# Six decay tiles spread by one-hot products into PSUM, a third chunk of masked float32 scores, and products of zeros at the start

## The chip, the cores and the metric

The kernel runs on one core of one Trainium2 chip. The metric is the device time of one execution in microseconds (us). Before the change its median over 3 runs is 554.11 us (554.05 to 554.75).

## The reference

Three stages follow each other: a scan-like attention over 32 sequences (4 batches by 8 heads, 768 positions, head size 32, state size 16), and two feed-forward layers over its 3072 tokens of width 256.

```python
# attention, chunk by chunk
cum = np.cumsum(log_a, axis=-1)
L = np.exp(cum[:, :, :, None] - cum[:, :, None, :]) * causal      # decay between two positions
y = (C @ B.T * L) @ x + (C @ state) * np.exp(cum)                  # within the chunk, and from before
state = decay_full * state + sum_j(B_j x_j * decay_from_j)
# first layer: 256 -> 768 -> 256
h = max(x @ w1, x @ w2, x @ w3);   x1 = h @ w_out
# second layer: 256 -> 1536 -> 256
out = (sigmoid(x1 @ w_gate) * (x1 @ w_val)) @ w_out2
```

All operands are float32, and the weights arrive as pairs of 32-bit words (int64 views on the host) that are decoded on the chip.

## The kernel before, in words

**Attention.** The kernel uses chunks of 96 positions (8 chunks) and handles four sequences at a time, so one chunk has 8 steps g and the whole attention 64 steps k. Step k does this:

- TensorE makes the scores `s` of four sequences, four matmuls of 128x96 into one PSUM bank. In the first `FIRST` = 16 steps (two chunks) both operands are float32: the columns of C are masked by ScalarE (`act.mul(ck ...)`, line 327) so that only the wanted sequence remains, and each float32 matmul stands in the trace as two records (line 332). Later chunks use bf16 parts: `split_bc` (line 294) loads B and C of the chunk, cuts them into three bf16 terms (ScalarE's casts in line 303, GpSimd's subtractions in line 312), and 12 DMAs put these into the tiles `bi` and `cs` (line 308). The matmul is then in line 335.
- `dec` holds the decay factors. One tile serves two steps. It is loaded from DRAM into all 128 partitions by a broadcast DMA of 388 KB (`load_decay`, line 269) and turned into running products by two scans on VectorE (`decay`, line 291) against a 0/1 matrix `delta` that lies in PSUM.
- VectorE multiplies scores by decay into `mt` (line 347), GpSimd adds 16 columns for the state (line 340), and TensorE makes `y` from `mt` and `xs` (line 356).
- When four steps are done, ScalarE and VectorE cut `y` into a high and a low part (`xt_hi` line 366, `xt_lo` line 368), and four VectorE transposes (line 372) put the new state into `xs` of the next chunk.

The first two `dec` tiles come straight from the input and are clipped on VectorE (line 287). The others come from `ad`, a clipped copy in DRAM that `clip_all` writes (lines 261 and 264).

**First layer.** The tokens are handled in 6 tiles t of 512. For each of 6 blocks m, three products `u` (j = 0, 1, 2; lines 406 to 408, each with a high and a low part) go into three PSUM banks. ScalarE copies the first (line 484), VectorE takes the maximum with the second and the third (lines 486 and 488), and a high and low part of that goes into the two products `o`. Block m needs the weight pieces `a{m}0` and `a{m}1`, 512 KB each. A piece is decoded by three ScalarE operations (lines 165, 170, 174), one VectorE operation `t_a` (line 178), one on GpSimd (line 183), a ScalarE copy (line 211) and a GpSimd subtraction (line 213).

**What sets the order.** All DMAs go through SyncE's queue in the order of issue. `BEHIND` ties the load of weight pieces to the load of a certain `dec` tile. A tile of `dec` can only be loaded when one of its `DECS` = 4 buffers is free. Twelve attention steps (`START`) run before the first layer begins with tile t = 0; they yield its 512 tokens. The other steps are spread between the products of the first layer (`UNTIL`: 24 steps done by the end of t = 0). Inside these bounds a scheduler puts each engine's instructions into their final order, and every engine takes its own strictly one after the other.

Of the kernel before, what the change touches and what calls it, by code (L numbers as in the profile page):

```python
# [19 lines left out]
CH = 96  # L20
# [22 lines left out]
FIRST = 2 * NG  # L43
MASKED = 8
SHARED = 24
LEAD = 2
# [6 lines left out]
BEHIND = {4: 1, 5: 1, 6: 2, 7: 2, 8: 2, 9: 1, 10: 1, 11: 1, 12: 1}  # L53
# [18 lines left out]
def scan_attention_then_ffn(ctx: ExitStack, tc: tile.TileContext, xh, ah, bch, pick, bn, w1, w2, w3,  # L72
# [62 lines left out]

    todo = [(piece1, m, part) for m in range(M1) for part in range(2)]
# [7 lines left out]
    def load_weights():  # L144
# [4 lines left out]
        for k, s in enumerate(loads):  # L149
            sp.dma_start(out=raw[:, 2 * k:2 * k + 2].rearrange("p b n t -> p b (n t)"), in_=s)  # L150
        loaded.append((raw, wpool, blocks, name))

    def decode(raw, wpool, blocks, name):
# [23 lines left out]
        with behind(1):  # L177
            dve.scalar_tensor_tensor(out=t, in0=f1, scalar=3, in1=sg, op0=ALU.logical_shift_left,
                                     op1=ALU.bitwise_or)
# [73 lines left out]
    bcf = [flat[:, MASKED * 4 * CH + (BW + 384) * k:][:, 0:BW + 384] for k in range(2)]  # L253
    pk = acon.tile([128, NG], F32, name="pk")

    def clip_all():

        t = awk.tile([128, 2, LW], F32, tag="ac", bufs=1, name="ac")
        sp.dma_start(out=t.rearrange("p u w -> p (u w)"),
                     in_=ah.rearrange("r (s w) -> (r s) w", s=4))  # L260
# [3 lines left out]
        sp.dma_start(out=ad.rearrange("r (s w) -> (r s) w", s=4),  # L264
                     in_=t.rearrange("p u w -> p (u w)"))
# [17 lines left out]
    def decay(n, clip=False):  # L283

        t = dec[n]
        if clip:
            dve.tensor_scalar(out=t[:, :, 1:LW], in0=t[:, :, 1:LW], scalar1=1e-6, scalar2=1.0,
                              op0=ALU.max, op1=ALU.min)
        for h in range(PU // 4):
            f = t[:, 4 * h:4 * h + 4].rearrange("p u w -> p (u w)")  # L290
            dve.tensor_tensor_scan(out=f, data0=f, data1=delta.rearrange("p u w -> p (u w)"),  # L291
                                   initial=0.0, op0=ALU.mult, op1=ALU.add)

    def split_bc(c):
# [6 lines left out]
        for p in range(3):  # L301
            with tc.issue_after(evict[0].ins) if c > 2 else ExitStack():
# [18 lines left out]
    def attention(k, ahead):  # L321
# [24 lines left out]
        else:  # L346
            last[0] = dve.tensor_tensor(out=m[:, :, 0:CH], in0=ps[:, :, 0:CH], in1=dc[:, :, 1:LW],
# [5 lines left out]
        for i in [g] if k < START else (g, g - 3, g - 2, g - 1) if g % 4 == 3 else []:  # L353
# [428 lines left out]
```

## Time and profile before

| | |
|---|---|
| median of 3 runs | 554.11 us |
| profiled execution | 554.77 us, span 553.0 us, so 1.77 us lie around the span |
| TensorE busy | 535.5 us (97%) |
| VectorE busy | 384.0 us (69%) |
| ScalarE busy | 322.2 us (58%) |
| GpSimd busy | 128.2 us (23%) |
| DMA | 50.51 MB, mean 91 GB/s over the span |

The shares are means over stages that differ. The profile is therefore read by stage below: the attention's first 12 steps (6.6 to 35.4 us), the first tile of the first layer (39.1 to 85.4 us), and what follows. In the trace PE is TensorE's matmuls, DVE is VectorE, ACT is ScalarE, POOL is GpSimd and SP is SyncE; a "q" behind a name is the engine's instruction queue. A matmul's duration includes its way through the array, so the distance from one start to the next tells its price in a row of equal ones. The column PEclk is the granted TensorE clock as a share of 2.4 GHz; before the first clock record, at 43.06 us, it shows 1.00 whatever the clock was.

### The profile page before, as it was taken

The page shows a single profiled execution, that of the slowest core. Times are in us where ns is not written, and L with a number is a line of the kernel's source. Part 1 is how long each engine was busy: PE and PEld are TensorE (multiplying, and loading weights), DVE is VectorE, ACT ScalarE, POOL GpSimd, SP SyncE. Part 2 cuts the span into 40 slices and gives each one's busy share as a digit, 9 for nine tenths or more (in the row PEclk, how much of TensorE's full clock was granted, in tenths as well). Part 3 has the DMA queues.
Part 4 walks back from the last instruction along what each step waited for, and adds up shares of the span by engine and source line. Part 5 has one row for each costly group of instructions (what it writes and reads, how often), then busy time and mean ns, then how long its engine had stood idle before and what let it go on. Part 6 is the DMA issues. An engine that isn't in the chain of part 4 may idle for free.

```text
span 553.0 us, 7923 instructions
## 1 busy us (share of the span) xinstructions
PE 535.5 (97%) x2885; PEld 429.3 (78%) x2885; DVE 384.0 (69%) x648; ACT 322.2 (58%) x571; POOL 128.2 (23%) x161
## 2 busy tenths in 40 slices
PE   5998999999999999999999999999999999999997
PEld 5777667777677778888888878877888878888885
DVE  4988985676776834799988896586455567554554
ACT  5667745334335223687798886675555565555563
POOL 3568996555555430000000000000000000000000
PEclk9999899999999999999999999999999999999999
DMA  7999985894985118013220000001000002000002
GB/s 234 344 268 241 298 200 87 187 180 142 192 197 125 31 59 321 1 38 118 76 75 0 1 1 2 0 19 58 1 0 2 0 1 77 0 1 0 1 0 76
DMA packets 32150, 50.51 MB, mean 91 GB/s; under 512 B 3184, under 2 KB 18160, under 8 KB 32112
## 3 DMA queue, kind: packets, MB, share of 16 engines
q1 hardware_dynamic: 31824, 49.63, 34.1%
q8 instruction: 22, 0.36, 0.3%
q10 hardware_dynamic: 288, 0.39, 0.2%
q14 instruction: 16, 0.13, 0.1%
HBM read 38.51 MB, written 3.25 MB: 76 GB/s over the span
## 4 chain that ended last, share of the span: by engine, by line
PE 83%; DMA 9%; DVE 4%; ACT 1%; issue 1%; SPq 0%; DVEq 0%; ACTq 0%
PE o L659 17%; PE ug L628 15%; PE uv L628 15%; PE u L406 9%; PE u L408 8%; PE u L407 8%; DMA raw_a<-in_w 6%; PE o L407 3%; PE o L406 3%; PE o L408 3%; DMA dec<-ad 2%; PE y L356 2%; PE s L335 1%; DVE dec L291 1%; DMA ad<-ac 1%
## 5 line engine op out<-in xcount | busy, mean ns | idle before, releaser
L659 PE MATMUL o<-hi,w_d 128*128 128x512 f32 x288 | 97.6, 390 | 0.0
L406 PE MATMUL u<-xt_hi,w_a 128*128 128x512 f32 x216 | 88.4, 409 | 3.7 <-DVE s L488 2.6
L628 PE MATMUL ug<-xt_hi,w_g 128*128 128x512 f32 x252 | 91.5, 392 | 0.1
L628 PE MATMUL uv<-xt_hi,w_v 128*128 128x512 f32 x252 | 90.3, 390 | 0.0
L407 PE MATMUL u<-xt_lo,w_a 128*128 128x512 f32 x216 | 85.8, 397 | 0.1
L408 PE MATMUL u<-xt_hi,w_a 128*128 128x512 f32 x216 | 85.5, 396 | 0.0
L659 PEld LDWEIGHTS o<-hi,w_d 128*128 128x128 f32 x288 | 54.0, 188 | 11.3 <-ACT hi L702 0.2
L703 DVE TENSOR_TENSOR lo<-y,hi 128x512 fp32r<-128x512 f32 x72 | 49.4, 688 | 16.8 <-ACT hi L702 15.9
L291 DVE TENSOR_TENSOR_SCAN dec<-dec,delta 128x388 f32<-128x388 f32 x64 | 57.8, 945 | 1.3 <-DMA dec<-ad 1.1
L477 ACT CAST hi<-s 128x512 fp32r<-128x512 f32 x36 | 22.3, 621 | 61.5 <-DVE s L488 60.9
L659 PE MATMUL o<-lo,w_d 128*128 128x512 f32 x144 | 56.4, 391 | 0.8 <-DVE lo L703 0.8
L628 PEld LDWEIGHTS ug<-xt_hi,w_g 128*128 128x128 f32 x252 | 47.3, 188 | 12.1 <-ACT ug L631 0.9
L628 PEld LDWEIGHTS uv<-xt_hi,w_v 128*128 128x128 f32 x252 | 47.3, 188 | 10.6 <-DVE y L699 0.8
L406 PEld LDWEIGHTS u<-xt_hi,w_a 128*128 128x128 f32 x216 | 41.2, 191 | 13.7 <-POOL mt L340 1.7
L628 PE MATMUL ug<-xt_lo,w_g 128*128 128x512 f32 x126 | 49.1, 390 | 0.0
L628 PE MATMUL uv<-xt_lo,w_v 128*128 128x512 f32 x126 | 49.0, 389 | 0.0
L408 PEld LDWEIGHTS u<-xt_hi,w_a 128*128 128x128 f32 x216 | 41.4, 192 | 9.1
L407 PEld LDWEIGHTS u<-xt_lo,w_a 128*128 128x128 f32 x216 | 41.3, 191 | 8.4 <-DVE xt_lo L368 0.6
L702 ACT CAST hi<-y 128x512 fp32r<-128x512 f32 x72 | 44.4, 620 | 5.8 <-DVE y L699 4.4
L699 DVE TENSOR_TENSOR y<-uv,y 128x512 f32<-128x512 f32 x36 | 24.8, 688 | 30.9 <-PE uv L628 30.7
L486 DVE TENSOR_TENSOR s<-u,s 128x512 f32<-128x512 f32 x36 | 24.8, 688 | 24.6 <-PE u L408 19.4
L636 DVE TENSOR_TENSOR y<-ug,y 128x512 f32<-128x512 f32 x36 | 24.8, 690 | 24.4 <-ACT y L633 17.4
(103 smaller groups left out, 956.9 us busy)
## 6 DMA issues: line engine op xcount, KB each, us to landing
dec<-ad SPq DMA_DIRECT2D x30, 388.0 KB, 5.8
raw_a<-in_w SPq DMA_DIRECT2D x18, 256.0 KB, 6.9
bi<-parts SPq DMA_DIRECT2D x36, 128.0 KB, 5.3
cs<-parts SPq DMA_DIRECT2D x36, 96.0 KB, 5.5
xs<-in_xh SPq DMA_DIRECT2D x6, 512.0 KB, 5.0
raw_g<-in_wg SPq DMA_DIRECT2D x6, 512.0 KB, 5.0
raw_v<-in_wv SPq DMA_DIRECT2D x6, 512.0 KB, 5.9
raw_d<-in_wo SPq DMA_DIRECT2D x6, 512.0 KB, 4.3
```

Of the source, the lines that this page charges most:

```text
L291: dve.tensor_tensor_scan(out=f, data0=f, data1=delta.rearrange("p u w -> p (u w)"), initial=0.0, op0=ALU.mult, op1=ALU.add)
L406: pe.matmul(ps, wlo, a_hi(k), start=k == 0, stop=False)
L407: pe.matmul(ps, whi, a_lo(k), start=False, stop=False)
L408: pe.matmul(ps, whi, a_hi(k), start=False, stop=k == kn - 1)
L477: act.copy(hl[0], s)
L486: dve.tensor_tensor(out=s, in0=banks[1], in1=s, op=ALU.max)
L628: turn[0] = pe.matmul(ps, w, x, start=new and e == 0, stop=e == 2, skip_group_check=not new)
L636: evict[1] = dve.tensor_tensor(out=self.t[k], in0=ps, in1=self.t[k], op=ALU.add)
L659: turn[0] = pe.matmul(acc2[t][d], w, x, start=n == 1 and e == 0, stop=n == M2 and e == 2)
L699: evict[1] = dve.tensor_tensor(out=g, in0=v, in1=g, op=ALU.mult)
L702: act.copy(hl[0], g)
L703: dve.tensor_tensor(out=hl[1], in0=g, in1=hl[0].bitcast(F32), op=ALU.subtract)
```

## The change

Six things are changed.

1. The first six `dec` tiles (`SPREAD`, 12 half tiles) are no longer loaded by broadcast DMAs. The clipped factors stay in a tile `a4`, one row for each half tile. A float32 product with a one-hot column (`spread`) copies row h to all 128 partitions of a PSUM bank, and the scan reads it there. Two banks, those of the later `o`, take turns: the product h + 2 follows the scan of h.
2. `FIRST` is 24: the third chunk's scores, too, are made from masked float32 operands, so `split_bc` starts with the fourth chunk.
3. At the very start 12 products of zeros (`idle_products`, bf16, 128x512) stand ahead of all other TensorE work; they read `sg`, which GpSimd clears first (line 142). Eight more follow steps 9, 10 and 11.
4. The weight pieces a00 and a01 are loaded ahead of the first `dec` tile that is still loaded, and two pieces ride behind each of the tiles 6 to 10.
5. VectorE's first decode operations are tied to attention steps (`AFTER`), and the `dec` tiles 6 and 7 are scanned after the twelfth step (`LATER`).
6. One step's state transposes are moved behind the low part of step 11, and `y` is made after each single step up to step 24.

```diff
-FIRST = 2 * NG
+FIRST = 3 * NG
+LATER = START // 2
+IDLE0 = 12
+IDLE = {9: 3, 10: 3, 11: 2}
+AFTER = {"a00": 6, "a01": 7, "a10": 11}
+SPREAD = 6
...
-BEHIND = {4: 1, 5: 1, 6: 2, 7: 2, 8: 2, 9: 1, 10: 1, 11: 1, 12: 1}
+BEHIND = {6: 2, 7: 2, 8: 2, 9: 2, 10: 2}
...
-        with behind(1):
-            dve.scalar_tensor_tensor(out=t, in0=f1, scalar=3, in1=sg, op0=ALU.logical_shift_left,
+        with behind(1) if second else tc.issue_after(mts[AFTER.get(name, -1)].ins):
+            mts[name] = dve.scalar_tensor_tensor(out=t, in0=f1, scalar=3, in1=sg,
...
+    a4 = acon.tile([128, 4, LW], F32, name="a4")
...
+        t = a4[0:NC * NP * 2]
+        dve.memset(a4[NC * NP * 2:128], 0.0)
...
+    def spread(h):
+
+        ps = pso.tile([128, TT], F32, tag=f"o{h % 2}", name=f"spread{h}")
+        pe.matmul(ps[:, 0:4 * LW], delta_s[:, 3, h + 1:h + 2].to_broadcast([128, 128]),
+                  a4.rearrange("p u w -> p (u w)"), start=True, stop=True)
+        spreads.append(ps)
...
-    def load_decay(n, src):
+    def load_decay(n):
         t = awk.tile([128, PU, LW], F32, tag="dec", bufs=DECS, name=f"dec{n}")
-        i = sp.dma_start(out=t.rearrange("p u w -> p (u w)"), in_=src[n].partition_broadcast(128))
         dec[n] = t
+        if n < SPREAD:
+            return
+        i = sp.dma_start(out=t.rearrange("p u w -> p (u w)"), in_=ad[n].partition_broadcast(128))
...
-        if clip:
-            dve.tensor_scalar(out=t[:, :, 1:LW], in0=t[:, :, 1:LW], scalar1=1e-6, scalar2=1.0,
-                              op0=ALU.max, op1=ALU.min)
         for h in range(PU // 4):
             f = t[:, 4 * h:4 * h + 4].rearrange("p u w -> p (u w)")
-            dve.tensor_tensor_scan(out=f, data0=f, data1=delta.rearrange("p u w -> p (u w)"),
+            a, d = (spreads.pop(0)[:, 0:4 * LW], delta_s) if n < SPREAD else (f, delta)
+            dve.tensor_tensor_scan(out=f, data0=a, data1=d.rearrange("p u w -> p (u w)"),
                                    initial=0.0, op0=ALU.mult, op1=ALU.add)
+            if 2 * n + h + 2 < 2 * SPREAD:
+                spread(2 * n + h + 2)
...
+    def idle_products(n, after=None):
+
+        ps = pso.tile([128, TT], F32, tag="o1", name=f"idle{after}")
+        z = sgs[1].rearrange("p b n -> p (b n)") if after is None else (
+            delta_s.rearrange("p u w -> p (u w)"))
+        z = z.bitcast(BF16)
+        for _ in range(n):
+            with tc.issue_after(mts[after].ins) if after is not None else ExitStack():
+                pe.matmul(ps, z[:, 0:128], z[:, 0:TT], start=True, stop=True)
...
+    idle_products(IDLE0)
...
-    load_decay(0, ah)
+    for n in range(4):
+        load_decay(n)
     constants()
+    for h in range(2):
+        spread(h)
```

How the instructions stand now is shown at three places. The first is TensorE's queue from its first matmul; `s_k` are scores, `y_106` is the bank of `y`. Before:

```order
L332 MATMUL s_0_171<-y_91 128x96 x4
L332 MATMUL s_1_177<-y_91 128x96 x4
L332 MATMUL s_2_183<-y_91 128x96 x4
L332 MATMUL s_3_191<-y_91 128x96 x4
L356 MATMUL y_106<-mt_98,xs_145 32x112 x4
L332 MATMUL s_4_208<-y_91 128x96 x4
```

Now, from the last of the twelve products of zeros:

```order
L436 MATMUL idleNone<-sg_88 128x512
L352 MATMUL s_0_190<-y_91 128x96
L281 MATMUL spread_160<-a_110,delta_s 128x388
L352 MATMUL s_0_190<-y_91 128x96 x3
L352 MATMUL s_1_196<-y_91 128x96 x4
L352 MATMUL s_2_202<-y_91 128x96
L281 MATMUL spread_162<-a_110,delta_s 128x388
L352 MATMUL s_2_202<-y_91 128x96 x3
L281 MATMUL spread_184<-a_110,delta_s 128x388
L352 MATMUL s_3_210<-y_91 128x96 x4
L376 MATMUL y_106<-mt_98,xs_164 32x112 x4
L281 MATMUL spread_187<-a_110,delta_s 128x388
```

Between the scores of two steps there stands now, from the third half tile on, one product of 388 columns.

The second place is VectorE's queue from its first operation. Before (line 287 is the clip, line 291 the scan, line 347 `mt`):

```order
L261 TENSOR_SCALAR ac<-ac 128x2x96
L287 TENSOR_SCALAR dec_116<-dec_116 128x8x96
L291 SCALAR_TENSOR_TENSOR dec_116<-dec_116,delta 128x388 x2
L287 TENSOR_SCALAR dec_149<-dec_149 128x8x96
L347 TENSOR_TENSOR mt_98<-s_0_171,dec_116 128x4x96
L347 TENSOR_TENSOR mt_99<-s_1_177,dec_116 128x4x96
L291 SCALAR_TENSOR_TENSOR dec_149<-dec_149,delta 128x388 x2
```

Now (line 309 is the scan, line 367 `mt`):

```order
L267 MEMSET a_110 64x388
L270 TENSOR_SCALAR a_110<-a_110 64x4x96
L309 SCALAR_TENSOR_TENSOR dec_130<-spread_160,delta_s 128x388
L367 TENSOR_TENSOR mt_98<-s_0_190,dec_130 128x4x96
L309 SCALAR_TENSOR_TENSOR dec_130<-spread_162,delta_s 128x388
L367 TENSOR_TENSOR mt_99<-s_1_196,dec_130 128x4x96
L309 SCALAR_TENSOR_TENSOR dec_131<-spread_184,delta_s 128x388
```

The clips of whole tiles are gone, and scan and `mt` take turns, one half tile at a time.

The third place is SyncE's DMA queue around the first weight pieces. Before:

```order
L269 DMA dec_162<-ad 128x776
L150 DMA raw_a_164<-in_w 128x2x256 x2
L269 DMA dec_219<-ad 128x776
L150 DMA raw_a_221<-in_w 128x2x256
L150 DMA raw_a_221<-in_wo 128x512
L280 DMA bx_325<-in_bn 128x512
L308 DMA bi_96<-parts_330 16x8x512
L269 DMA dec_250<-ad 128x776
```

Now:

```order
L156 DMA raw_a_176<-in_w 128x2x256 x2
L156 DMA raw_a_179<-in_w 128x2x256
L156 DMA raw_a_179<-in_wo 128x512
L300 DMA xs_172<-in_xh 128x512
L300 DMA bx_173<-in_bn 128x256
L412 DMA y_91<-in_bch 128x896
L317 DMA bc_691<-in_bch 128x896
L290 DMA dec_272<-ad 128x776
```

The first piece stands before the seventh `dec` tile, which is now the first that is loaded at all, and no parts of the third chunk are written.

## Rows read from the trace of the kernel before

**Rows 1.** Busy by stage: stretch, PE, PEld, DVE, ACT, POOL, PEclk, DMA share, GB/s.

```profile
6.60:35.40 28.80, 28.75 (x192) 24.18 (x192) 23.98 (x39) 16.58 (x29) 12.46 (x19) 1.00 1.01 306
35.40:39.10 3.70, 2.92 (x14) 2.32 (x11) 3.62 (x7) 2.54 (x5) 2.27 (x3) 1.00 0.98 283
39.10:85.40 46.30, 42.45 (x284) 32.51 (x285) 39.25 (x63) 29.10 (x50) 41.62 (x40) 0.96 0.91 238
85.40:126.00 40.60, 40.60 (x295) 31.03 (x294) 27.11 (x46) 17.66 (x30) 23.98 (x28) 1.00 0.89 168
126.00:551.00 425.00, 420.80 (x2107) 339.30 (x2105) 289.68 (x494) 251.82 (x451) 44.05 (x55) 1.00 0.18 51
```

**Rows 2.** A group of first-layer products, 6.6 to 85.4 us; idle time before it behind the bar.

```profile
L408 PE MATMUL u<-xt_hi,w_a 128*128 128x512 f32 x36 | 15.3, 425 | 0.0
```

**Rows 3.** Chain that ended last, in order of time: start, us, what.

```profile
22.54 9.89 DMA raw_a<-in_w
...
46.53 6.87 DMA raw_a<-in_w
```

**Rows 4.** Timeline of TensorE: start, us, engine, line, operation; merged rows carry a count.

```profile
6.65 7.22 PE L332 MATMUL s<-y 128*128 128x96 f32 x32 [6.65 <-DMA y<-in_bch]
...
26.24 0.60 PE L356 MATMUL y<-mt,xs 128*32 128x112 f32 x8
...
28.73 0.60 PE L356 MATMUL y<-mt,xs 128*32 128x112 f32 x8
...
33.70 1.72 PE L356 MATMUL y<-mt,xs 128*32 128x112 f32 x32
...
40.12 0.63 PE L406 MATMUL u<-xt_hi,w_a 128*128 128x512 f32 x1
40.55 0.63 PE L407 MATMUL u<-xt_lo,w_a 128*128 128x512 f32 x1
...
43.32 1.03 PE L332 MATMUL s<-y 128*128 128x96 f32 x8
44.13 0.48 PE L406 MATMUL u<-xt_hi,w_a 128*128 128x512 f32 x1
...
53.34 0.97 PE L356 MATMUL y<-mt,xs 128*32 128x112 f32 x32
54.43 0.51 PE L335 MATMUL s<-cs,bi 96*128 96x96 bf16 x8
```

**Rows 5.** Groups on VectorE, 6.6 to 85.4 us, with idle time before each.

```profile
L291 DVE TENSOR_TENSOR_SCAN dec<-dec,delta 128x388 f32<-128x388 f32 x28 | 25.3, 946 | 1.3 <-DMA dec<-ad 1.1
L178 DVE SCALAR_TENSOR_TENSOR t_a<-raw_a,sg 128x512 int32<-128x512 int32 x12 | 13.4, 1119 | 0.1
L347 DVE TENSOR_TENSOR mt<-s,dec 128x384 f32<-128x384 f32 x24 | 12.8, 543 | 2.0 <-PE s L332 1.9
...
L486 DVE TENSOR_TENSOR s<-u,s 128x512 f32<-128x512 f32 x6 | 4.1, 690 | 5.0 <-PE u L408 4.4 <-ACT raw_a L170 0.6
...
L368 DVE TENSOR_TENSOR xt_lo<-y,xt_hi 128x384 fp32r<-128x384 f32 x6 | 3.3, 547 | 1.5 <-ACT xt_hi L366 1.5
L287 DVE TENSOR_SCALAR dec<-dec 128x768 f32<-128x768 f32 x2 | 1.1, 560 | 3.9 <-DMA dec<-in_ah 3.9
```

**Rows 6.** Timeline of the start on GpSimd and VectorE, columns as in rows 4.

```profile
0.74 0.99 POOL L142 MEMSET sg<- 128x512 int32 x2 [0.29 <-POOLq L767]
...
7.66 0.56 DVE L287 TENSOR_SCALAR dec<-dec 128x768 f32<-128x768 f32 x1 [3.35 <-DMA dec<-in_ah]
```

**Rows 7.** DMA issues: destination, queue, count, KB each, median us to landing.

```profile
dec<-ad SPq DMA_DIRECT2D x30, 388.0 KB, 5.8
...
bi<-parts SPq DMA_DIRECT2D x36, 128.0 KB, 5.3
cs<-parts SPq DMA_DIRECT2D x36, 96.0 KB, 5.5
```

**Rows 8.** A group on ScalarE, 6.6 to 85.4 us, columns as in rows 5.

```profile
L327 ACT ACTIVATE y<-y,pk 128x384 f32<-128x384 f32 x11 | 6.2, 604 | 6.1 <-DMA y<-in_bch 4.6 <-PE s L332 1.4
```

More of the change, by code (lines that the diff above doesn't have):

```diff
@@ L301, in split_bc @@
         for p in range(3):
-            with tc.issue_after(evict[0].ins) if c > 2 else ExitStack():
+            with tc.issue_after(evict[0].ins) if evict[0] else ExitStack():
                 act.copy(parts[:, p], r)
@@ L346, in attention @@
         else:
-            last[0] = dve.tensor_tensor(out=m[:, :, 0:CH], in0=ps[:, :, 0:CH], in1=dc[:, :, 1:LW],
+            last[0] = mts[k] = dve.tensor_tensor(out=m[:, :, 0:CH], in0=ps[:, :, 0:CH], in1=dc[:, :, 1:LW],
                                         op=ALU.mult)
@@ L352, in attention @@
         lead = None
-        for i in [g] if k < START else (g, g - 3, g - 2, g - 1) if g % 4 == 3 else []:
+        for i in [g] if k < SHARED else (g, g - 3, g - 2, g - 1) if g % 4 == 3 else []:
             for q in range(4):
@@ L367, in attention, with turn @@
             yield
-            dve.tensor_tensor(out=lo, in0=src, in1=hi.bitcast(F32), op=ALU.subtract)
-            if c + 1 < NC:
-                for q in range(4):
-                    rows = slice(32 * q, 32 * q + 32)
-                    dve.transpose(
-                        out=xs[c + 1][rows, 16 * h:16 * h + 16, :].rearrange(
-                            "p (g q) d -> p g q d", q=4)[:, :, q, :],
-                        in_=y[rows, :, CH:128])
+            i = dve.tensor_tensor(out=lo, in0=src, in1=hi.bitcast(F32), op=ALU.subtract)
+            if k + 1 == START:
+                mts[-1] = i
+                with tc.issue_after(i.ins):
+                    turn(0, 1, ys[1])
+            if c + 1 < NC and k != 7:
+                turn(c, h, y)
+    def turn(c, h, y):
+        for q in range(4):
+            rows = slice(32 * q, 32 * q + 32)
+            dve.transpose(
+                out=xs[c + 1][rows, 16 * h:16 * h + 16, :].rearrange(
+                    "p (g q) d -> p g q d", q=4)[:, :, q, :],
+                in_=y[rows, :, CH:128])
     def prepare(k):
@@ L381, in prepare @@
             load_x(c + 1)
-            splits.append(split_bc(c + 1))
+            if c + 1 < FIRST // NG:
+                with tc.issue_after(mts["load a01"].ins):
+                    sp.dma_start(out=bcf[c + 1], in_=bch[:, c + 1])
+            else:
+                splits.append(split_bc(c + 1))
         if splits and next(splits[0], None) is splits:
@@ L532, in scan_attention_then_ffn @@
             att_step(LEAD)
-        if k == 4:
-            load_x(1, slice(16, 32))
+        if k == 6:
+            with tc.issue_after(mts["load a01"].ins):
+                load_x(1, slice(16, 32))
         pipe.tick()
+        if k == 10:
+            weights_tick()
+            weights_tick()
+        if k - LEAD - 1 in IDLE:
+            idle_products(IDLE[k - LEAD - 1], k - LEAD - 1)
     for _ in range(9):
@@ L538, in scan_attention_then_ffn @@
         weights_tick()
+    for n, name in enumerate((-1, "a10")):
+        with tc.issue_after(mts[name].ins):
+            decay(LATER + n)
     slots = 4 * M1
```

42 lines of the change are left out of this document (21 added, 21 removed).

## The prediction

> **What bounds the kernel now.** I read the busy time by stage first, because the page's 97% for TensorE says nothing about where it could be shorter [rows 1]. From 126 us on TensorE is busy 420.80 of 425.00 us, and from 85.4 to 126 us all the time. What comes after 85.4 us is therefore TensorE's own work, which the change does not touch, and the end moves with the moment at which the first layer's tile t = 0 is done: its 3 x 6 banks take two products of each kind, and the 36th of line 408 stands before 85.4 us [rows 2]. Ahead of it are two stages. In the attention's first 12 steps TensorE also seems full (28.75 of 28.80 us). The timeline shows at what rate: one step takes 2.49 us (28.73 - 26.24), and the 32 score records from 6.65 us take 7.22 us, 0.22 us each [rows 4]. The same eight records take 1.03 us at 43.32 us, with the next product starting 0.81 us after them, so 0.10 us each. So the clock was half as fast in the first stage: 1.2 GHz until about 43 us, where the clock column has no record. Products of 512 columns stand 0.43 us apart there (40.12 us), which makes 0.21 us at 2.4 GHz. The third view is the chain that ended last: from 22.54 to 53.40 us it is one weight load after the other [rows 3]. In t = 0, then, three things meet: late weights, a TensorE that is at 1.2 GHz for part of the time (mean granted clock 0.96), and VectorE, busy 39.25 of 46.30 us, beside GpSimd with 41.62 [rows 1]. The change lightens the DMA, moves the clock, and leaves VectorE nearly all its work. That is the core of my forecast.
>
> **DMA.** Ahead of the weight pieces go six broadcasts of 388 KB and, for the third chunk, six writes of 128 KB and six of 96 KB [rows 7]: 2328 + 1344 = 3672 KB or 3.76 MB. (The chunk's own 448 KB are loaded either way.) At the 306 GB/s of the first stage [rows 1] these are 12.3 us, and the pieces can land that much earlier. That is a bound of the gain and not the gain, since other engines are late next.
>
> **The zeros at the start.** They can begin when `sg` is cleared, at 0.74 + 0.99 = 1.73 us [rows 6]; 12 at 0.43 us end at 6.9 us. The first score started at 6.65 us, waiting for its operands from DRAM [rows 4], so the zeros cost 0.2 us at most. If they were not there, nothing else would run on TensorE. What they may bring is the clock. No row shows whether zeros raise it; dense 512-column products at 40 us were followed by the full clock by 43.3 us, and the float32 scores and `y`, 28 us without a gap, were not. The Trainium skill ("TensorE: Matmul & The Clock Gate", Part 1) says that the throttled state is the default and activity releases it; here the trace agrees for dense products and disagrees for the scores, although their records fill the time. By the page alone the scores keep the full clock once it is up, and the sum below holds. The rows leave open whether they do, and that is the third rival.
>
> **The spread products.** The trace has no float32 product of 388 columns. The nearest are the `y` products of 112 columns, four side by side, two records each: 32 records take 0.97 us at full clock and 1.72 us at half [rows 4], that is 8 starts. At half clock 8 records alone take 0.60 us, so six more starts take 1.72 - 0.60 = 1.12 us, 0.19 us each, and half that, 0.10, at full clock. For 388 columns and two records: 2 x 388/112 x 0.10 = 0.70 us at full, 1.3 us at half clock. From below, at the rate of the 512-column products (0.21 us at full clock), it is 0.33 us; from above, with 0.97/8 per start, 0.84. I take 0.70, since `y` has the same operand type. A step on TensorE is then 0.85 (scores) + 0.25 (`y`) + 0.70 = 1.8 us at full clock instead of 2.49.
>
> **VectorE in the attention.** A step needs one half-tile scan of 0.946 us and one `mt` of 0.543 us, 1.49 us [rows 5]. I count the scan from PSUM at the same price: before, its other operand came from PSUM. If the swap cost or saved a tenth, 12 scans would give 1.1 us either way. The first scan needs one score and one spread product behind the zeros, so it starts at 8.0 us (before, at 7.66 + 0.56 = 8.2 us [rows 6]). For about seven steps TensorE's 1.8 us set the pace and VectorE idles 7 x 0.3 = 2.2 us; then come decode, transposes and low parts on VectorE, which makes it the slower one. Its list up to the twelfth `mt` is 12 scans, 12 `mt`, two `t_a`, two low parts and four short transposes: 11.4 + 6.5 + 2.2 + 1.1 us and about one more, 22 us. The twelfth `mt` ends at about 8.0 + 22 + 2 = 32 us, and t = 0 begins at 33.4 us instead of 39.1 us.
>
> **TensorE in t = 0.** The third chunk's scores become float32: 8 steps at 0.85 instead of 0.25 us (eight bf16 records of two steps take 0.51 us [rows 4]), about +5 us. ScalarE gets 8 maskings of 0.604 us [rows 8] and loses three casts; GpSimd loses two subtractions. ScalarE is busy 29.10 of 46.30 us, so I count nothing; if it were late each time, its 8 x 0.6 = 4.8 us would be the price. The products of zeros behind steps 9 to 11 are 8 x 0.21 = 1.7 us in a place where TensorE waits for the low part; I count nothing, and 1.7 us as the upper end.
>
> **The sum.** VectorE is busy 23.98 us in the first stage, 39.25 us in t = 0 and 3.6 us between them, 66.8 us in the 78.8 us from 6.6 to 85.4 us [rows 1]. It is idle 12.0 us, 10.9 of them behind the start of its first clip at 7.66 us [rows 6]. The change takes off two clips, 2 x 0.56 us [rows 5], and leaves 65.7 us, for as many scans, `mt`, decode steps and maxima stand in its list up to t = 1 as before. From 8.0 us without a gap it would end at 73.7 us. Of the old idle time, the waits for `dec` (1.3 us), for scores (2.0 us) and part of the 5.0 us for `u` go [rows 5]; I put 2.2 us (TensorE's pace, above), 1.5 us for the low parts as before and 4.0 us for `u`: 7.7 us. t = 0 ends at 81.4 us instead of 85.4 us, 4.0 us earlier. The profiled execution took 554.77 us (553.0 and 1.77 around it), 0.66 more than the median; with the same 4.0 us it would be 550.8, and the median 554.11 - 4.0 = 550.1 us. With 3 us of idle time left it would be 545.4, with all 10.9 us of it 553.3.
>
> **Rivals.**
> 1. *Weights alone bound t = 0.* The chain speaks for it [rows 3]. Then the whole 12.3 us would come: 541.8 us. Against it: VectorE had only 7 us to spare in the 46.30 us of t = 0 [rows 1], and TensorE gets 5 us more. TensorE's own content of t = 0 is 42.45 us busy, less 46.3 x 0.04 = 1.9 us and 2 us up to 43 us for the half clock, plus 5: 43.5 us; from 33.4 us it would end at 76.9 us and give 545.6 us. Together 0.09, most of it near 545.
> 2. *What the DMA gives, t = 0 gives back.* The float32 scores (+5 us), the transposes and four scans that now lie behind step 11 eat the earlier start of 5.7 us; VectorE keeps its 10.9 us of idle time. 553 to 555 us. For it speaks that the same engines are full in the same stage; against it that the waits for late weights go. Chance 0.16.
> 3. *The clock stays at half through the attention.* Zeros do not raise it, or scores, `y` and spreads do not hold it; the rows show 28 us of such work at 1.2 GHz. Then a step is 2.49 + 1.3 = 3.8 us, twelve are 15.6 us longer than before, and t = 0 begins at about 52 us instead of 39 us. It then has its weights, and VectorE is ahead, but TensorE alone needs 43.5 us and some 2 us until the clock is up: it ends near 98 us, 13 us later, 567 us. The point from which it decides: a step longer than 2.49 us. For the opposite speaks that at 43 to 50 us scores between 512-column products kept the full clock [rows 4], and that a step at full clock now leaves TensorE hardly a gap. Chance 0.14.
>
> **How the numbers follow.** The forecast (VectorE bounds the way to the end of t = 0, at the full clock) has 0.61 and its own range is 546 to 553 us. With rival 1 below and rivals 2 and 3 above, 546 to 556 us leaves out about 0.2: most of rival 3 and the lower part of rival 1. Faster by over 0.2% (below 553.0 us, about what a measurement of this kernel can tell) has 0.59 of the forecast, all of rival 1 and 0.06 of rival 2: 0.74. Within 0.2% are 0.02 and 0.08: 0.10. Slower: 0.02 of rival 2 and rival 3, 0.16.
>
> **What would show it.** Right: the eight score records of a step take about 1 us from the start; the twelfth `mt` ends near 32 us; VectorE is over 90% busy from 8 to 80 us; the chain ahead of t = 1 runs over VectorE instead of weight loads; the stretch behind t = 0 is as long as before. Wrong: score records 0.22 us apart (rival 3); weight loads still last in the chain; t = 0 longer than 49 us.

## The result and the profile after

The changed kernel takes 559.65 us (median of 6 runs, 558.95 to 561.12). The kernel before, run beside it on the same chip, takes 555.01 us (6 runs, 554.05 to 556.67). The ratio is 1.0087 with a 95% interval of 1.0066 to 1.0109: slower by 4.6 us where 4 us faster were forecast, and above the range.

Busy time by stage of the changed kernel, with the columns of [rows 1]: the attention's twelve steps, the way to t = 0, t = 0, t = 1, and the rest.

```profile
6.60:33.90 27.30, 26.68 (x210) 18.30 (x209) 21.37 (x31) 17.57 (x33) 8.25 (x15) 1.00 0.93 311
33.90:37.50 3.60, 3.38 (x25) 1.95 (x26) 2.95 (x8) 2.85 (x5) 1.58 (x2) 1.00 0.62 172
37.50:90.00 52.50, 49.55 (x322) 37.51 (x321) 43.00 (x69) 30.21 (x52) 41.56 (x42) 0.97 0.61 153
90.00:130.00 40.00, 40.00 (x293) 30.54 (x292) 26.41 (x46) 17.79 (x30) 23.98 (x29) 1.00 0.89 179
130.00:556.00 426.00, 420.41 (x2106) 339.09 (x2104) 289.54 (x494) 251.48 (x450) 43.96 (x55) 1.00 0.18 50
```

The attention is hardly shorter than before, and t = 0 is over 6 us longer: TensorE is busy 49.55 us in it, not 42.45 us. From 90 us on nothing has changed. The DMA engines fell from 238 to 153 GB/s in t = 0. So the relief came, but it had little to give: TensorE stood idle for only 46.30 - 42.45 = 3.85 us of t = 0 before, and for 2.95 us now.

The marks used below are the first, the 37th and the 73rd `u` record of the third kind (line 408 before, line 449 after), which start t = 0, t = 1 and t = 2. Counting up to t = 2 matters: each kernel makes 66 `o` products in these two tiles, but some make 30 of them in t = 0 (the changed kernel among them) and some 26 (the kernel before).

| | start of t = 0 | t = 0 | t = 0 and t = 1 | span |
|---|---|---|---|---|
| before | 39.70 | 46.36 | 86.54 | 553.0 |
| after | 37.94 | 52.69 | 91.97 | 556.7 |
| difference | -1.76 | +6.33 | +5.43 | +3.7 |

The first answer to where the time went is TensorE's groups in t = 0 (idle time before a group behind the bar), of the kernel before and then of the changed one.

```profile
L332 PE MATMUL s<-y 128*128 128x96 f32 x24 | 3.2, 276 | 1.0 <-DVE s L488 1.0
L356 PE MATMUL y<-mt,xs 128*32 128x112 f32 x96 | 2.9, 262 | 0.0
L335 PE MATMUL s<-cs,bi 96*128 96x96 bf16 x32 | 2.4, 208 | 0.1
```

```profile
L352 PE MATMUL s<-y 128*128 128x96 f32 x88 | 12.5, 290 | 1.3 <-ACT s L525 1.3
L376 PE MATMUL y<-mt,xs 128*32 128x112 f32 x96 | 5.0, 281 | 0.0
```

Scores go from 3.2 + 2.4 to 12.5 us of busy time, and the same 96 records of `y` from 2.9 to 5.0 us. These records lap over each other. Counted from one start to the next, without the idle time between, the whole of t = 0 and t = 1 adds up like this:

| us from start to start | before | after | difference |
|---|---|---|---|
| scores | 6.05 | 12.68 | +6.63 |
| `y`, 192 records each | 5.50 | 6.87 | +1.37 |
| `u` and `o`, 281 records each | 71.14 | 69.47 | -1.67 |
| TensorE idle | 3.85 | 2.95 | -0.90 |
| sum | 86.54 | 91.97 | +5.43 |

`u` and `o` got cheaper although they are as many: in the kernel before the clock was at half for 6.8 us of t = 0 (up to 43.06 us and from 56.7 to 60.1 us), in the changed kernel for 3.4 us. The new products took more than that saving and the saved idle time together.

The chain of waits over t = 0 says whether TensorE had room for them. Here is its summary, first of the kernel before (39 to 86 us), then of the changed one (44.3 to 90 us).

```profile
by line: DMA raw_a<-in_w 30.7%; PE u L406 12.3%; PE u L407 11.0%; PE u L408 10.7%; DVE s L488 4.2%; DVE dec L291 3.8%; DVE t_a L178 2.8%; PE o L406 2.7%; issue 2.6%; PE o L407 2.5%; ACT raw_a L170 2.5%; PE o L408 2.4%; DVE xs L372 2.2%; PE 
```

```profile
by line: PE s L352 22.7%; PE u L447 19.6%; PE u L449 16.7%; PE u L448 16.6%; PE y L376 9.1%; PE o L447 6.0%; PE o L448 5.2%; PE o L449 4.5%
```

The weight loads [rows 3] are gone from the chain, as forecast. What stands in their place from 44.2 us on is TensorE alone, not VectorE. Ahead of that TensorE waits twice, 1.29 us for a ScalarE copy and 1.66 us for an `mt` of VectorE.

The second answer is why the start gained so little. The timeline of TensorE shows three steps of the attention, at full clock; lines 352, 376 and 281 are scores, `y` and the spread product.

```profile
23.92 1.13 PE L352 MATMUL s<-y 128*128 128x96 f32 x8
24.98 0.38 PE L376 MATMUL y<-mt,xs 128*32 128x112 f32 x2
25.29 0.92 PE L281 MATMUL spread<-a,delta_s 128*128 128x388 f32 x2
26.14 0.39 PE L376 MATMUL y<-mt,xs 128*32 128x112 f32 x6
26.46 1.13 PE L352 MATMUL s<-y 128*128 128x96 f32 x8
27.52 0.40 PE L376 MATMUL y<-mt,xs 128*32 128x112 f32 x8
27.85 0.92 PE L281 MATMUL spread<-a,delta_s 128*128 128x388 f32 x2
28.61 1.03 PE L352 MATMUL s<-y 128*128 128x96 f32 x8
29.57 0.40 PE L376 MATMUL y<-mt,xs 128*32 128x112 f32 x8
```

A step takes 26.46 - 23.92 = 2.54 us where the spread stands between two parts of `y`, and 2.05 us where it doesn't (27.52 to 29.57). Before it took 2.49 us at half the clock. So the doubled clock was eaten by the new product and by changes from one kind of product to the next: a part of `y` with 2 records takes 0.31 us to the next start, the whole group of 8 elsewhere 0.33 us. VectorE's groups from 6.6 to 90 us show who waited:

```profile
L309 DVE TENSOR_TENSOR_SCAN dec<-spread,delta_s 128x388 f32<-128x388 f32 x12 | 11.5, 961 | 7.3 <-PE spread L281 7.1
```

### The profile page after: what moved, and what is told of

It is laid out like the page before. It is cut to its first block, busy times and chain, and to the rows that moved or that the text cites. A ratio compares the mean times of both kernels' runs of the same rounds, so it can differ in the third digit from the quotient of the medians.

```text
span 556.7 us, 8015 instructions
## 1 busy us (share of the span) xinstructions
PE 544.8 (98%) x2960; PEld 429.2 (77%) x2961; DVE 384.0 (69%) x647; ACT 324.4 (58%) x576; POOL 123.2 (22%) x159
## 4 chain that ended last, share of the span: by engine, by line
PE 87%; DVE 3%; ACT 1%; issue 1%; DMA 0%; DVEq 0%; ACTq 0%
PE o L712 17%; PE ug L681 15%; PE uv L681 15%; PE u L447 9%; PE u L448 8%; PE u L449 8%; PE o L447 3%; PE o L448 3%; PE o L449 3%; PE y L376 2%; PE s L352 2%; PE s L355 1%; DVE dec L309 1%; DVE xs L400 0%; DMA out_t<-y 0%
## 5 line engine op out<-in xcount | busy, mean ns | idle before, releaser
L447 PEld LDWEIGHTS u<-xt_hi,w_a 128*128 128x128 f32 x216 | 40.6, 188 | 12.3 <-DVE mt L367 1.8
L449 PEld LDWEIGHTS u<-xt_hi,w_a 128*128 128x128 f32 x216 | 40.7, 188 | 8.9
L309 DVE TENSOR_TENSOR_SCAN dec<-dec,delta 128x388 f32<-128x388 f32 x52 | 46.8, 943 | 0.0
```

The lines of the kernel that those rows point to most:

```text
L309: dve.tensor_tensor_scan(out=f, data0=a, data1=d.rearrange("p u w -> p (u w)"), initial=0.0, op0=ALU.mult, op1=ALU.add)
L447: pe.matmul(ps, wlo, a_hi(k), start=k == 0, stop=False)
L449: pe.matmul(ps, whi, a_hi(k), start=False, stop=k == kn - 1)
```

## The experiments

Theory A: TensorE's own time sets both stages, through the step's price up to t = 0 and through float32 scores and single `y` steps in t = 0. The rivals are that VectorE or late weights set the start or the end (B), that the one-hot products cost more than the scores (C, D), that the traffic itself and not a queue's order makes weights late (T). Each run is compared with the kernel before on its own chip; that kernel's medians there lie between 554.57 and 555.67 us.

### Which part costs: e8, e1, e9

e8 puts the third chunk's float32 scores alone into the kernel before.

```diff
-FIRST = 2 * NG
+FIRST = 3 * NG
...
-            splits.append(split_bc(c + 1))
+            if c + 1 < FIRST // NG:
+                sp.dma_start(out=bcf[c + 1], in_=bch[:, c + 1])
+            else:
+                splits.append(split_bc(c + 1))
```

> The kernel before, with one part of the change alone: the third chunk's scores are made from float32 operands, loaded directly, in place of bf16 parts written out and read back (the decay tiles are still broadcast by DMA, no zeros). Theory A (this part is what costs in t = 0: 32 float32 scores for 32 of bf16, some 5 to 6 us of TensorE there, of which the traffic saved gives back some): slower than before by 1 to 4 us, with (0,0,0) beginning earlier than 39.7 and t = 0 longer than 46.4 us. Theory C (the cost comes with the one-hot products, and this part pays for itself by 1.3 MB less DMA): no slower than before, 0 to 3 us faster.

Measured: 560.86 us, 1.0102 [1.0080, 1.0124]. This part alone makes the kernel as slow as the whole change does: from the start of t = 0 (38.52) to t = 2 it takes 93.59 us, 7.1 more than before. Not all of that is the scores' own price, for a wait came with them. In t = 0 TensorE stands idle for 4.4 us until a `dec` tile has landed (the scan on VectorE waits 5.39 us for it), and runs at half clock from 65.9 to 72.7 us:

```profile
62.80 0.40 PE L411 MATMUL o<-hi,w_a 128*128 128x512 f32 x1
67.59 0.79 PE L409 MATMUL u<-xt_hi,w_a 128*128 128x512 f32 x1 [4.40 <-DVE mt L347]
```

```profile
65.27 1.81 DVE L291 TENSOR_TENSOR_SCAN dec<-dec,delta 128x388 f32<-128x388 f32 x2 [5.39 <-DMA dec<-ad]
```

The loss is more than the 1 to 4 us that Theory A forecast, and Theory C is out.

e1 takes this part out of the changed kernel.

```diff
-FIRST = 3 * NG
+FIRST = 2 * NG
```

> The changed kernel with the third chunk's scores from bf16 parts again (FIRST = 16); all else as changed. Theory A (TensorE's own work in t = 0 sets the end: 88 float32 score records at 0.11 us and some at half clock, against 24 and 32 bf16 records of 0.05 us before): t = 0 gets 6 us shorter, 553 to 555 us. Theory B (VectorE sets the end, because four scans and four transposes moved behind step 11): the scores' type hardly matters, 558.5 to 560 us. If the additional DMA traffic (1.34 MB, 4 to 5 us at 300 GB/s) makes weights late again, something between.

Measured: 558.66 us, 1.0072 [1.0048, 1.0095], hardly better. Start to t = 2 falls by 4.2 us to 87.77, but t = 0 starts at 42.01 instead of 37.94. The time lies in the range of Theory B and the cause is not B's, for the chain is weight loads again and not VectorE:

```profile
22.07 5.37 DMA raw_a<-in_w
27.45 8.78 DMA raw_a<-in_w
36.25 6.59 DMA raw_a<-in_w
```

SyncE's queue shows why those are late (start, us, line, operation): it stands at the first transfer of the parts, with the weight loads queued behind.

```profile
12.85 0.33 SPq L317 DMA_DIRECT2D bc<-in_bch  x1
20.25 0.63 SPq L328 DMA_DIRECT2D bi<-parts  x1
20.93 0.59 SPq L290 DMA_DIRECT2D dec<-ad  x1
21.57 1.47 SPq L156 DMA_DIRECT2D raw_a<-in_w  x3
```

e9 therefore takes out the price and nothing else.

```diff
-            if k < FIRST:
+            if k < 2 * NG:
...
+            elif k < FIRST:
+                b, x = (v.bitcast(BF16).rearrange("p (n t) -> p n t", t=2)[:, :, 1] for v in (
+                    bcf[c][:, 128 * q:128 * q + 128], ck[:, q]))
+                pe.matmul(ps[:, q, 0:CH], b, x, start=True, stop=True)
```

> The changed kernel, but the eight steps of the third chunk make their scores in one bf16 pass from the upper halves of the same masked float32 operands (so those scores have bf16 precision only; nothing else differs: same loads, same masking, no parts). It takes out TensorE's price of float32 scores in t = 0 and nothing else: 64 records of 0.11 us become 32 shorter ones. Theory A (that price, paid on a TensorE that has no slack in t = 0, is what made the change slower): t = 0 some 5 to 6 us shorter than the 52.7 us of the changed kernel, time 553 to 555, no slower than the kernel before. Theory D (the one-hot products and singly issued y are the main cost): t = 0 at most 2 us shorter, time 557 to 559.

Measured: 555.19 us, 1.0006 [0.9987, 1.0025]. Theory A holds, and D is out: the float32 price of one chunk's scores is 0.81% or 4.5 us by the two ratios (their intervals leave some 1.6 us either way). The groups of scores in t = 0 (38.5 to 87.4 us) beside the 12.5 us above:

```profile
L352 PE MATMUL s<-y 128*128 128x96 f32 x24 | 4.4, 343 | 1.3 <-ACT s L529 1.3
L357 PE MATMUL s<-y 128*128 128x96 bf16 x32 | 2.4, 207 | 0.0
```

### The zeros: e3, e4

e3 leaves out all products of zeros of the changed kernel.

```diff
-IDLE = {9: 3, 10: 3, 11: 2}
+IDLE = {}
...
-    idle_products(IDLE0)
```

> The changed kernel without any products of zeros (12 at the start, 8 behind steps 9 to 11). If the zeros are what raised the clock (full from 7.5 us on): the attention's steps run at 1.2 GHz, 3.5 to 4.5 us each instead of 2.54, and the time is 570 us or more. If scores, y and spread products would raise it by themselves: within 1 us of the changed kernel, 558.5 to 560.5 us.

Measured: 558.37 us, 1.0071 [1.0044, 1.0098]: the same as with them, within the intervals. The first spreads then run at half clock, and the clock is full from 11.65 us on:

```profile
6.05 2.85 PE L281 MATMUL spread<-a,delta_s 128*128 128x388 f32 x4
8.69 3.56 PE L352 MATMUL s<-y 128*128 128x96 f32 x18
12.09 0.84 PE L281 MATMUL spread<-a,delta_s 128*128 128x388 f32 x2
```

Two spreads take 2.85 us at half clock; one takes 0.84 us at full.

e4 puts the twelve zeros at the head of the kernel before.

```diff
+    idle_products(12)
     sp.dma_start(out=pk, in_=pick)
```

> The kernel before with only the 12 products of zeros ahead of its TensorE work. Its attention step took 2.49 us at 1.2 GHz, all of it TensorE. If zeros raise the clock and it holds: a step falls to what VectorE and the decay loads allow, 1.6 to 2.0 us, the attention ends at 28 to 31 us instead of 35.4 us; the weights are as late as before, so 2 to 4 us of this remain: 551 to 553 us. If the first layer waits for weights all the same: 554 to 555 us, as before.

Measured: 558.88 us, 1.0062 [1.0035, 1.0088], slower, which neither forecast allowed. The profiled execution (554.34 us) does run at full clock from 7.7 to 21.4 us. In this stretch TensorE waits twice for `mt`, 3.6 us in all; then the clock falls to half for 10 us, and after the last `y` TensorE waits for weights:

```profile
29.55 1.72 PE L356 MATMUL y<-mt,xs 128*32 128x112 f32 x32
35.76 0.79 PE L413 MATMUL u<-xt_hi,w_a 128*128 128x512 f32 x1 [4.49 <-POOL w_a L213]
```

Without the change's other parts the clock brings t = 0 forward (36.78 instead of 39.70), but t = 0 and t = 1 take 88.94 instead of 86.54 us: eight more score records lie behind the mark, and the clock is at half for 8.5 us of it instead of 6.8. The twelve executions differ in the granted clock: its mean was 0.981 in the two that took 554.03 and 554.34 us, and 0.966 to 0.972 in the ten that took 557.52 to 559.93 us. Where those ten were at half clock no profile shows.

### The price of changing kinds: e2, e5, e6, e7, e7b

e2 makes `y` in batches of four groups again from step 12 on.

```diff
-        for i in [g] if k < SHARED else (g, g - 3, g - 2, g - 1) if g % 4 == 3 else []:
+        for i in [g] if k < START else (g, g - 3, g - 2, g - 1) if g % 4 == 3 else []:
```

> The changed kernel with y made for four steps at once from step 12 on, as before the change, instead of after each step up to 24. Theory A: a group of eight y records costs 0.33 us and the product behind it 0.2 us more; in fours the same costs 0.95 us for 32; t = 0 gets 1 to 2 us shorter, 557.5 to 558.5 us. Theory B: no difference (559 to 560 us).

e5 moves the spread behind the `y` of its step.

```diff
-                spread(2 * n + h + 2)
+                if n:
+                    due.append(2 * n + h + 2)
+                else:
+                    spread(2 * n + h + 2)
...
+        while due and i_y is not None:
+            with tc.issue_after(i_y.ins):
+                spread(due.pop(0))
```

> The changed kernel, but each one-hot product of the decay (from the second tile on) is issued behind the y records of its attention step and no longer between two groups of them. Theory A (the price of TensorE's step sets when t = 0 begins: the step took 2.54 us with the product between the y records and 2.04 us without): about 0.3 us less in five steps, the first u some 1 to 2 us earlier than 35.8, time 1 to 2 us below the changed kernel's. Theory B (VectorE's scans or the weights set the beginning, TensorE's steps lie beside them): no change, within 0.5 us of the changed kernel, the scans at most 0.3 us later each.

e6 makes the spread from two one-pass products: its operands are a high and a low part of type fp32r, and each product then stands in the trace as one record.

```diff
+        dve.tensor_copy(a4r[0], a4)
+        dve.tensor_tensor(out=a4r[1], in0=a4, in1=a4r[0].bitcast(F32), op=ALU.subtract)
...
-        pe.matmul(ps[:, 0:4 * LW], delta_s[:, 3, h + 1:h + 2].to_broadcast([128, 128]),
-                  a4.rearrange("p u w -> p (u w)"), start=True, stop=True)
+        for k in range(2):
+            pe.matmul(ps[:, 0:4 * LW], one[:, h + 1:h + 2].to_broadcast([128, 128]),
+                      a4r[k].rearrange("p u w -> p (u w)"), start=k == 0, stop=k == 1)
```

> The changed kernel, but the six decay tiles are spread by two one-pass products of 388 columns (a high and a low part, cut by VectorE once at the start, some 1 us there) in place of one float32 product of two records of 0.42 us. Theory A (TensorE's step price sets the beginning): about 0.4 us less in each of twelve products, the first one 1 us later, together 2 to 4 us less by the first u, time 2 to 3 us below the changed kernel's. Theory B (VectorE or weights set it): no gain, and the cut on VectorE costs up to 1 us.

e7 joins all three, e7b joins e2 and e6 (the text on e7 says step 8; its batches of four begin at step 12, like those of e2).

> The changed kernel with the two edits of e5 and e6 and, from step 8 on, y in batches of four groups again as in e2, so TensorE changes its kind of product less often. Theory A (what TensorE is given up to the end of t = 0 sets the time): the gains add, 2 to 3 us (e2) and 2 to 4 us (e5, e6): 551 to 554, no slower than the kernel before. Theory B: what e2 gave stays and nothing comes on top, 556 to 557.

> The changed kernel with e2 (y in batches of four groups from step 12) and e6 (spread in two one-pass products). If their gains add: 553 to 555. If the beginning is set by what else it waits for once TensorE is ahead (as e7 hinted): 556 to 557, as each alone.

| | median | ratio | start of t = 0 | start to t = 2 | half clock up to t = 2, us |
|---|---|---|---|---|---|
| after | 559.65 | 1.0087 [1.0066, 1.0109] | 37.94 | 91.97 | 45.0-48.5 |
| e2 | 556.32 | 1.0032 [1.0014, 1.0049] | 39.14 | 88.71 | none |
| e5 | 557.18 | 1.0037 [1.0021, 1.0053] | 36.59 | 90.84 | none |
| e6 | 557.01 | 1.0033 [1.0020, 1.0047] | 35.66 | 91.29 | none |
| e7 | 556.59 | 1.0035 [1.0014, 1.0057] | 40.49 | 89.73 | 25.8-39.5, 46.3-49.7 |
| e7b | 555.71 | 1.0010 [0.9991, 1.0030] | 35.23 | 89.16 | 40.2-43.6 |

Theory A is right on the start: e5 touches nothing but the order of TensorE's step, e6 makes the spread cheaper and even adds two operations on VectorE, t = 0 starts 1.4 and 2.3 us earlier, and each takes some 3 us off the time. (The rest of these 3 us lies behind the start, where the profile of the changed kernel has 3.4 us of half clock and theirs none.) Theory B is out as the only bound. e2 takes 3.1 us off by the ratios, more than the 1 to 2 us forecast. VectorE's wait for spreads falls from 7.1 us to 3.0 us in e6, for an equal number of scans:

```profile
L315 DVE TENSOR_TENSOR_SCAN dec<-spread,delta_s 128x388 f32<-128x388 f32 x12 | 11.2, 955 | 3.2 <-PE spread L287 3.0
```

Between e5 and e2, both at full clock throughout, the batches of four are worth 90.84 - 88.71 = 2.1 us; what e5 moves, the spreads, all lies ahead of the start. The group of `y` in e2's t = 0 is back at its old price:

```profile
L376 PE MATMUL y<-mt,xs 128*32 128x112 f32 x96 | 2.9, 262 | 0.0
```

In e7b the gains add in part: the sum of e2's and e6's would be a ratio of 0.998, and 1.0010 was measured, the level of the kernel before. e7 gives no more than e2 alone, the forecast of its Theory B. But the profile of e7, an execution of 558.92 us, has 13.7 us of half clock ahead of t = 0, and its twelve executions follow the granted clock: the six with a mean of 0.993 to 0.996 took 554.98 to 556.10 us, the level of e7b, the two with 0.990 took 557.07 and 557.54 us, and the four with 0.981 to 0.985 took 558.92 to 560.01 us. So e7's missing gain goes with lost clock in half of its executions; what loses the clock there is not shown.

### Can the early start be kept with bf16 parts: e11, e13 to e17

e11 and e13 go back to bf16 parts for the third chunk and make them three steps later (on e6 and on e7b).

```diff
-FIRST = 3 * NG
+FIRST = 2 * NG
+SPLIT = 3
...
-            else:
+            elif c > 1:
                 splits.append(split_bc(c + 1))
+        if c == 1 and g == SPLIT:
+            splits.append(split_bc(c + 1))
```

> e6 (decay spread in two one-pass products) with the third chunk's scores from bf16 parts again, but the parts made three steps later (from step 11 and not step 8), so that SyncE issues the weights of the first three row blocks before it waits for the parts. Theory A: the beginning of t = 0 stays where e6 has it (35.7 for the first whole u, not 42.0 as with the parts made at step 8 in e1) and t = 0 takes some 47 to 48 us as in e1, not 52: 551 to 553, faster than the kernel before by 2 to 4 us. Theory D or a new wait (the parts come too late for step 16, or block later weights): t = 0 keeps 50 us or more, 555 to 558.

> e11 with y in batches of four groups from step 12 on again, as the kernel before has it. Theory A (each change of kind of product costs TensorE about 0.2 us, twelve steps in t = 0): 1 to 2 us less than e11, 550 to 552. Otherwise equal to e11 within 1 us, or later by what the masked products then wait for the fourth mt.

Measured: 563.86 us, 1.0162 [1.0140, 1.0184], and 562.62 us, 1.0143 [1.0120, 1.0167]. e11 is slower than either of its forecasts, and e13 is 1.2 us below it. The start is kept (36.82 and 36.18), and the wait stands in t = 0 instead, where the parts arrive too late. In e11 SyncE issues the last of them at 57.72 us, and the bf16 scores begin at 65.45 us (the trace puts the wait down to the next chunk's load `bc`, issued behind them):

```profile
56.55 0.73 PE L456 MATMUL o<-hi,w_a 128*128 128x512 f32 x2
65.45 0.80 PE L362 MATMUL s<-cs,bi 96*128 96x96 bf16 x8 [8.16 <-DMA bc<-in_bch]
```

e14 to e17 leave the time of the parts and let ScalarE issue their transfers: e14 in e1, e15 and e16 with the spreads of e6 and e7b, e17 in the kernel before.

```diff
-                        sp.dma_start(
+                        (act if c == 2 else sp).dma_start(
```

> e1 (the changed kernel, third chunk from bf16 parts) with the twelve transfers of that chunk's parts issued by ScalarE and not SyncE; traffic unchanged. Theory Q (SyncE's order made the weights late: it stood 7.5 us at the first parts with the weight loads behind): the loads of the second and third row block issue some 6 us earlier, t = 0 begins at 37 to 39 in place of 42.0 and takes 47 to 49 us: 553 to 555. Theory T (the traffic itself): the weights land as late as in e1, t = 0 begins at 41 to 42, 558 to 559.

> e14 with the spread in two one-pass products (e6). Theory Q and A together: begins 1 to 2 us before e14, 551 to 554, below the kernel before. Theory T: 556 to 558.

> e15 with y in batches of four groups from step 12 on. If changes of kind on TensorE cost t = 0 anything beside the scores: 1 to 2 us below e15, 550 to 553; otherwise equal to e15 within 1 us.

> The kernel before with the same edit: the third chunk's parts issued by ScalarE. Theory Q: SyncE's order holds weights there too (they end its chain at 22.5 and 46.5 us), so some of the 39.1 us before t = 0 goes: 552 to 554. If the DMA engines and not the order set that kernel's start: no change, within 1 us of before.

Measured: e14 561.90 us, 1.0120 [1.0092, 1.0148]; e15 559.62, 1.0079 [1.0050, 1.0109]; e16 560.48, 1.0094 [1.0066, 1.0122]; e17 571.73, 1.0281 [1.0241, 1.0322]. e14, e15 and e17 missed what either theory said; e16 is level with e15 within 1 us, its second forecast. SyncE does issue the next weights earlier in e14 (15.02 instead of 21.57 us), but now ScalarE stands at the parts, and ScalarE decodes the weights. Its longest waits in e17, from 8 to 50 us (the second is in the kernel before too, with 4.6 us):

```profile
ACT parts L303 <- DMA cs<-parts: 6.0, 1, 6.0
ACT y L327 <- DMA y<-in_bch: 5.5, 1, 5.5
ACT parts L303 <- DMA raw_a<-in_w: 3.0, 1, 3.0
```

So the test did not separate Q from T: the wait moved to an engine where it costs more. That is left open; what is shown is that in each place tried the changed kernel with bf16 parts was no faster than with float32 scores, within the intervals, or slower.

### The sum: e10, e20

e10 joins e6 and e9, e20 joins e7b and e9 (the third chunk's scores have bf16 precision in both).

> e6 and e9 together: cheaper spread, and the third chunk's scores in one bf16 pass from the upper halves of the float32 operands (those scores then have bf16 precision only). Theory A: e6's 2.5 us and e9's 4.5 us add: 552 to 553, below the kernel before by 2 to 3 us. If the earlier start is worth nothing: 555, level with e9.

> e10 with y in batches of four groups from step 12 on. If changes of kind on TensorE still cost something once the scores are cheap: 1 to 2 us below e10; otherwise level with it.

Measured: 553.72 us, 0.9972 [0.9954, 0.9991], and 552.14 us, 0.9944 [0.9924, 0.9965]. Both are faster than the kernel before, and the gains add within the intervals: e6's and e9's would make a ratio of 0.9952 in e10, whose time is 0.7 us above Theory A's range. The one-pass scores take 0.61% off from e6 to e10 and 0.66% from e7b to e20, 3.4 and 3.7 us, and e20 lies 1.6 us below e10, as forecast. e20's t = 0 from 35.7 to 81.9 us, to be read against 49.55 us of PE in the changed kernel:

```profile
35.70:81.90 46.20, 41.86 (x287) 31.49 (x286) 40.61 (x68) 30.51 (x52) 41.34 (x42) 0.96 0.74 171
```

Start to t = 2 is 86.43 us, that of the kernel before (86.54), from a start 3.6 us earlier. So the early start is real time, worth 3 us, once TensorE is given next to nothing more to do in t = 0. With whole float32 values e7b is the best of these: it equals the kernel before and does not beat it.

## Why the prediction was wrong

**What held.** The clock came up at 7.50 us and held up to 45.05 us; score records stand 0.11 us apart, eight to 0.9 us. The first scan starts at 8.3 us (8.0 predicted), weight loads left the chain, and from t = 1 on nothing changed. VectorE's own list was sized right (67.3 us busy from 8.3 to 90 us, 65.7 predicted). Rival 3 is out, and so is rival 1.

**The step that failed: "VectorE bounds the way to the end of t = 0".** From VectorE's first scan to the end of t = 0 TensorE is busy 77.92 us and VectorE 67.31 us (columns as in [rows 1]):

```profile
8.30:90.00 81.70, 77.92 (x549) 56.42 (x549) 67.31 (x106) 48.94 (x85) 51.38 (x59) 0.98 0.71 204
```

VectorE stands idle for 14.4 of the 81.7 us, not for 7.7. From 8 to 80 us it is 84% busy where over 90% was to be the sign of being right, and the sign of being wrong came: t = 0 is longer than 49 us. The step rests on two terms for TensorE, both too small.

1. *The step at 1.8 us.* It took 2.54 us, and 2.05 us where the spread did not split `y`. From start to start the spread takes 0.85 us (0.76 where it does not split `y`), not 0.70, the scores 1.06 us (0.96), not 0.85, and `y` 0.63 us in two parts (0.33 in one), not 0.25. The upper bound of 0.84 was the right one for the spread, and a single group of `y` cannot be priced by its share of a row of equal ones. VectorE then waited 7.1 us for spreads, not 2.2, and the twelfth `mt` ended at 34.6 us instead of 32. The way from there on was too short as well. The prediction's 39.1 us is the start of the first `u` with a low part; the changed kernel has it at 37.52 us, 2.9 us behind the twelfth `mt` and not 1.4, and TensorE is busy nearly all that time, with scores, `y` and products of zeros. So t = 0 started 1.6 us earlier than before by this mark, 1.8 us by the one in the table, instead of 5.7.

2. *TensorE in t = 0.* The prediction put TensorE's own content of t = 0 at 43.5 us at full clock, with "about +5 us" for the scores in it, and hid it behind VectorE. The cover was not there: of the 52.5 us VectorE is busy 43.0 and TensorE 49.55, with 3.4 us at half clock; e6, all at full clock, has 48.59 us. So the term was some 5 us too small. The scores were sized nearly right (from e6 to e10 they take 5.4 us less). What has no price in the sum is `y` after each single step, the sixth of the changes (TensorE is busy 48.53 us in e5's t = 0 and 45.38 us in e2's, 3.2 us less), and the four `o` products that moved forward from t = 1, some 0.9 us.

What the two costs are worth in time can be read from two pairs with TensorE at full clock in t = 0 and t = 1: 91.29 - 88.00 = 3.3 us for the scores (e6 to e10) and 2.1 us for `y` (e5 to e2). Both are less than the 5.4 and 3.2 us that TensorE is spared, because it then waits longer for VectorE (its idle time grows from 3.4 to 5.0 us and from 3.0 to 4.1 us). In e10's t = 0 VectorE is busy 43.26 us and TensorE 42.81 us: there the cover begins that the prediction counted on from the start. That 3.3 + 2.1 us is also the growth of 5.43 us in the tables is partly chance, for the changed kernel saved half clock and idle time too. With the start at -1.76 us the growth leaves +3.7 us, the difference of the spans.

**Rival 2** ("What the DMA gives, t = 0 gives back") named the right place, and with the float32 scores one of the costs, at a chance of 0.16. It stopped at 553 to 555 us because it still let t = 0 start 5.7 us early and took its time from VectorE's idle time. Its four scans behind step 11 show too: TensorE's wait of 1.66 us up to 44.23 us is for an `mt` that stands behind the scans of the `dec` tiles 6 and 7, one piece of 3.52 us on VectorE. The wait of 1.29 us ahead of it ends with a ScalarE copy, which stood behind work that waited for VectorE's `t_a`, and that for eight transposes. The kernel before has even more idle time in t = 0 (3.85 against 2.95 us).

**Costed at nothing.** The zeros: rightly so for the time, but they are not the only thing that gave the clock, for without them it was full from 11.65 us on (e3).

**Not tried.** No run takes out the new order of the weight loads, the ties of VectorE's decode or the late scans by themselves, so what these parts cost or give stays open.

## What to carry to other kernels

When a change takes away what bounds a stage, first add up each other engine's own time in that stage, start to start and with the change's additions in it: what is put on the engine that comes out longest is paid for the most part (here 5.4 of 8.6 us), whatever another engine was expected to cover. A product that stands alone between products of other shapes costs more than its share of a row of equal ones, so batches are worth keeping even where the data would be ready sooner. Moving a blocked transfer to another queue moved the wait here, and it got worse because that queue's engine feeds the path. And a single profile shows one execution: where executions of one kernel differ by several us, compare their granted clocks before adding up gains.

## What the runs showed of the hardware

- **The clock of the same work differs between kernels and between executions.** In the profile of the kernel before, the 32 score records at the head and what followed them, 28.75 us of work in 28.80 us, ran at half clock. In e8, which has the same 32 records there, the clock was full from 11.28 to 24.93 us, with no zeros and no spreads: 24 records still take 0.21 us each, and eight then 1.10 us together. Here are the rows of e8, against the first 32 of before in 7.22 us [rows 4]:

```profile
6.89 4.98 PE L332 MATMUL s<-y 128*128 128x96 f32 x24 [6.89 <-ACT y L327]
12.51 1.10 PE L332 MATMUL s<-y 128*128 128x96 f32 x8 [0.64 <-DVE mt L347]
```

  The Trainium skill ("TensorE: Matmul & The Clock Gate", Part 1) says that the throttled state is the default and activity releases it; e8 and e3 agree, while in the one profile of before 28.75 us of work did not release it. So the "28 us of such work at 1.2 GHz", on which the third rival rests, were one execution and no rule. Nor is the kernel before one case: in 26 executions beside e10 its mean granted clock lay between 0.977 and 1.000.
- **A short group of `y` costs nearly the same whatever its length.** At full clock, between other products, 2, 6 and 8 records take 0.31, 0.32 and 0.33 us to the start of the next product (the rows from 24.98 us on above). In a row of 32, eight take 0.24 us (0.97 us [rows 4]).
- **A float32 product against two one-pass ones.** Between two parts of `y`, 388 columns take 26.14 - 25.29 = 0.85 us as a float32 product (two records, in the changed kernel) and, as two one-pass products, 15.74 - 15.19 = 0.55 us in e6, to the start of the next product in both:

```profile
15.19 0.44 PE L287 MATMUL spread<-a4hi,one 128*128 128x388 f32 x1
15.47 0.34 PE L287 MATMUL spread<-a4lo,one 128*128 128x388 f32 x1
15.74 0.39 PE L382 MATMUL y<-mt,xs 128*32 128x112 f32 x6
```
